# Spectral layers: the order of sum and split behind the second transform, and the rest's sum at the step's end

## The chip, the cores and the metric

One NeuronCore of a Trainium2 chip runs the whole program. The metric is the device time of one execution in microseconds. The engines are TensorE (PE in the profile, matrix products), VectorE (DVE), ScalarE (ACT), GpSimd (POOL) and SyncE (SP, which here only issues transfers). Each works off its own queue in order. Matrix products are written into PSUM, eight banks of 512 float32 per partition; ScalarE and VectorE read them from there.

## The reference, cut to what matters

Two inputs of 4096 tokens with 640 features go through a Fourier transform over tokens and features, a two-layer network on the complex spectrum in four blocks of 160 features, and the inverse transform. A gated feed-forward layer on the same tokens is mixed in.

```python
Xf = rfft2(x, axes=(1, 2))                     # x: (2, 1, 4096, 640)
z = Xf.reshape(B, H, Wf, 4, 160); zr, zi = z.real, z.imag
hr = zr @ w1[0] - zi @ w1[1] + b1[0]           # per block
hi = zi @ w1[0] + zr @ w1[1] + b1[1]
hr, hi = relu(hr), relu(hi)
or_ = hr @ w2[0] - hi @ w2[1] + b2[0]
oi_ = hi @ w2[0] + hr @ w2[1] + b2[1]
or_, oi_ = softshrink(or_, 0.01), softshrink(oi_, 0.01)
a = irfft2(or_ + 1j * oi_, s=(H, W), axes=(1, 2))
b = (gelu(x @ w_gate) * (x @ w_up)) @ w_down
g = sigmoid((x * gate_w).sum(-1, keepdims=True))
out = g * a + (1 - g) * b
```

The kernel takes a complex product as three real ones, for which it needs the sum of real and imaginary part beside the parts themselves. [...]

## The kernel before, in words

The program has three stages in time: the gated layer's first products, with the first transform between them; the spectral layers; and the second product of the gated layer, with the inverse transform and the output. The change lies in the spectral layers and in the last piece of the first stage, which prepares them.

The spectrum is cut into 16 chunks of 256 frequencies (eight for each input; chunk (0, 0), the second in order, has 258 and is called wide), and each chunk into its four blocks. A step is one block of one chunk: 64 steps in all. Of a block's 160 features 128 are the main part, and the remaining 32 of all four blocks together make a tile of 128, called the rest, which is treated once for a chunk and goes through memory to be read back block by block (zl).

fwd2 is the second half of the forward transform. Four products of TensorE fill one PSUM bank, pz, with real and imaginary parts (pr[:, 0] and pr[:, 1], 256 columns each). ScalarE rounds both into the high part z (high, L292 by the profile), and copies the second component into a buffer zt (L1030). VectorE subtracts the high part from the bank for the low part (low, L295) and adds the bank's first component to zt (L1033). fwd2 returns a function that splits that sum into zs, high on ScalarE and low on VectorE.

main_z calls fwd2 for a step's main part, one step ahead of its use; rest calls it for the rest and calls the returned function at once, then hands the parts to st, which puts stores off into a list (late) that flush issues on SP's queue at the start of the next step. zl_load, two steps ahead of use, reads them back on the same queue.

mlp1 is the first layer: products of zs into a bank (copied to kc by ScalarE, L1118), products of z, two additions hs on VectorE (L1125), then the function that main_z returned for the next step (so zs of the next step is split here), then relu and split of hs into h (L1081 on ScalarE, L1082 on VectorE), the last 32 features (L1131 on ScalarE, L1132 on VectorE), and in the end their split (L1135, L1136 and L1137), which mlp1 returns as a function called more. mlp2 is the second layer (m on ScalarE, y on VectorE). y_split splits y after every second step, its second half on GpSimd; inv1 is the inverse transform's first product, also after every second step, whose results go from PSUM to the buffer is, half of them by ScalarE (L1198), half by VectorE (L1200).

Nothing plans the order: each engine takes its instructions in the order of the code. One pass i of the loop over the steps issues, in this order: a load of the next chunk (in some steps), the flush of late, rest (once a chunk, in steps 4 ch - 3, two steps earlier for the last chunk), zl_load, main_z of step i + 1, mlp1 of step i, mlp2 of step i - 1, more of step i, inv1 of an earlier pair of steps if i is odd, y_split if i is even. The first chunk's rest is called in the last piece of the first stage.

Buffers come from pools with names: tiny (15 buffers of 1280 bytes a partition), small (17 of 2560), big (29 of 5120) and bank (8 PSUM banks). A tile takes a buffer that an earlier one has left; if the work on that one isn't over, the first writer waits. Where two engines touch the same tile or the same bank, semaphores keep them in the code's order.

## Time and profile before

| | |
|---|---|
| median of 3 runs | 2449.84 us (2448.95 to 2451.41) |
| profiled execution, its time | 2452.71 us |
| its span, first to last instruction | 2450.9 us |
| granted TensorE clock, mean | 0.996 |
| busy: TensorE, VectorE, ScalarE, GpSimd | 98%, 81%, 60%, 7% |
| stretch 1330 to 1742 us (spectral layers): TensorE, VectorE, ScalarE, GpSimd busy | 391.06, 343.70, 324.12, 77.20 of 412 us |

The profile is one execution on the chip. A row of the timeline gives start, duration (both us), engine, line, operation, the tiles written and read, their shape, and in brackets how long the engine had been idle before it and which instruction of another engine ended that. A row of the waits gives who waited for whom, the sum in us, how often, and the longest. The engines are named PE, DVE, ACT, POOL and SP; PEld is TensorE's loading of weights, which overlaps its products. L292 and L295 are the lines of the helpers high and low, L314 of the helper for a group of products, so such rows are told apart by their tiles.

### The profile page before, as it was taken

The page shows a single profiled execution, that of the slowest core. Times are in us where ns is not written, and L with a number is a line of the kernel's source. Part 1 is how long each engine was busy: PE and PEld are TensorE (multiplying, and loading weights), DVE is VectorE, ACT ScalarE, POOL GpSimd, SP SyncE. Part 2 cuts the span into 40 slices and gives each one's busy share as a digit, 9 for nine tenths or more (in the row PEclk, how much of TensorE's full clock was granted, in tenths as well). Part 3 has the DMA queues.
Part 4 walks back from the last instruction along what each step waited for, and adds up shares of the span by engine and source line. Part 5 has one row for each costly group of instructions (what it writes and reads, how often), then busy time and mean ns, then how long its engine had stood idle before and what let it go on. Part 6 is the DMA issues. An engine that isn't in the chain of part 4 may idle for free.

```text
span 2450.9 us, 50023 instructions
## 1 busy us (share of the span) xinstructions
PE 2413.5 (98%) x17983; PEld 2394.3 (98%) x17983; DVE 1984.5 (81%) x4191; ACT 1477.0 (60%) x3368; POOL 169.3 (7%) x270
## 2 busy tenths in 40 slices
PE   9999999999999999999999999999999999999999
PEld 9999999999999999999999999998899999999999
DVE  7777778777778888888757888888888988888887
ACT  5544456655556666666546777777745555555554
POOL 0111110000000000000001121211000000000000
PEclk9999999999999999999999999999999999999999
DMA  5666576777777768677765566668964455555443
GB/s 214 243 233 228 221 257 210 260 253 251 259 260 247 255 227 271 234 272 239 250 246 173 171 196 187 200 194 258 319 187 150 151 152 159 168 162 160 152 145 104
DMA packets 341314, 521.78 MB, mean 213 GB/s; under 512 B 28862, under 2 KB 217926, under 8 KB 341066
## 3 DMA queue, kind: packets, MB, share of 16 engines
q1 hardware_dynamic: 321002, 465.30, 57.7%
q0 software_dynamic: 20064, 53.29, 6.0%
q8 instruction: 142, 2.33, 0.4%
q14 instruction: 106, 0.87, 0.1%
HBM read 323.17 MB, written 195.30 MB: 212 GB/s over the span
## 4 chain that ended last, share of the span: by engine, by line
PE 86%; DMA 4%; DVE 4%; ACT 3%; issue 1%; SPq 1%; DVEq 0%; ACTq 0%
PE bank L580 73%; PE bank L314 7%; PE bank L711 2%; PE bank L834 1%; DMA zl<-zl 1%; PE bank L1018 1%; DMA sc<-scr 1%; DMA scr<-is 1%; DVE hs L1125 1%; ACT h L1081 1%; ACT ys L292 1%; DVE zt L1033 1%; ACT z L292 1%; DVE h L1082 1%; DMA xraw<-in_xT_dram 0%
## 5 line engine op out<-in xcount | busy, mean ns | idle before, releaser
L580 PE MATMUL bank<-xo,w 128*128 128x320 f32 (+1 forms) x9000 | 1252.5, 298 | 4.5 <-ACT u L607 3.6
L580 PEld LDWEIGHTS bank<-xo,w 128*128 128x128 f32 x9000 | 1221.8, 189 | 6.1 <-ACT u L607 3.8
L580 PE MATMUL bank<-wx,ho 128*128 128x320 f32 x4608 | 634.1, 300 | 3.4 <-DMA wx<-wdf 3.4
L580 PEld LDWEIGHTS bank<-wx,ho 128*128 128x128 f32 x4608 | 629.5, 189 | 4.3 <-DMA wx<-wdf 4.1
L295 DVE TENSOR_TENSOR ho<-hraw,ho 128x640 fp32r<-128x640 f32 (+3 forms) x384 | 194.4, 541 | 28.7 <-ACT ho L292 26.2
L292 ACT ACTIVATE ho<-hraw 128x640 fp32r<-128x640 f32 x320 | 169.0, 571 | 41.5 <-PE bank L580 31.3
L607 ACT ACTIVATE u<-bank 128x320 f32<-128x320 f32 (+1 forms) x250 | 107.5, 430 | 139.8 <-PE bank L580 133.6
L657 DVE TENSOR_TENSOR u<-bank,u 128x320 f32<-128x320 f32 (+1 forms) x165 | 80.1, 485 | 87.1 <-ACT u L607 86.1
L295 DVE TENSOR_TENSOR xs<-xr,xs 64x640 fp32r<-64x640 f32 x128 | 105.0, 820 | 47.0 <-ACT xs L292 43.7
L836 DVE TENSOR_TENSOR as<-bank,as 64x320 f32<-64x320 f32 x256 | 113.8, 484 | 25.6 <-ACT as L835 23.8
L295 DVE TENSOR_TENSOR xo<-xraw,xo 128x640 fp32r<-128x640 f32 (+1 forms) x155 | 125.1, 807 | 8.5 <-ACT xo L292 6.6
L314 PE MATMUL bank<-wm,h 128*128 128x320 f32 (+1 forms) x792 | 130.7, 301 | 0.1
L607 ACT ACTIVATE p<-bank 128x320 f32<-128x320 f32 (+1 forms) x125 | 54.1, 433 | 119.8 <-PE bank L580 61.8
L835 ACT ACTIVATE as<-bank 64x320 f32<-64x320 f32 x256 | 96.6, 426 | 31.7 <-PE bank L834 28.6
L292 ACT ACTIVATE xo<-xraw 128x640 fp32r<-128x640 f32 (+1 forms) x155 | 111.7, 721 | 5.9 <-DMA xraw<-in_xT_dram 4.1
L314 PEld LDWEIGHTS bank<-wm,h 128*128 128x128 f32 (+1 forms) x792 | 113.1, 188 | 1.5 <-ACT wt L1118 0.4
L1419 ACT ACTIVATE bank<-bank 128x320 f32<-128x320 f32 x31 | 13.1, 422 | 168.3 <-PE bank L580 168.3
L1413 DVE SCALAR_TENSOR_TENSOR uu<-bank,gs,uu 128x320 f32<-128x320 f32 x193 | 102.7, 546 | 13.0 <-PE bank L580 9.5
L1385 DVE SCALAR_TENSOR_TENSOR uu<-bank,gs,uu 128x320 f32<-128x320 f32 x120 | 57.8, 545 | 48.9 <-ACT uu L1384 48.8
L292 ACT ACTIVATE xs<-xr 64x640 fp32r<-64x640 f32 x128 | 93.4, 730 | 2.8 <-DMA hD<-h 0.7
L608 ACT ACTIVATE h<-bank 128x320 f32<-128x320 f32 (+1 forms) x165 | 71.2, 432 | 36.0 <-PE bank L580 33.0
L607 ACT ACTIVATE pb<-bank 128x320 f32<-128x320 f32 x80 | 35.0, 437 | 88.7 <-PE bank L580 88.6
(188 smaller groups left out, 3590.6 us busy)
## 6 DMA issues: line engine op xcount, KB each, us to landing
xo<-xD SPq DMA_DIRECT2D x96, 640.0 KB
xraw<-in_xT_dram SPq DMA_DIRECT2D x158, 320.0 KB
hD<-h SPq DMA_DIRECT2D x128, 320.0 KB
hraw<-hD SPq DMA_DIRECT2D x128, 320.0 KB
xD<-xo POOLq DMA_DIRECT2D x48, 640.0 KB, 4.3
sc<-scr SPq DMA_DIRECT2D x65, 320.0 KB
xr<-in_x_dram SPq DMA_DIRECT2D x64, 320.0 KB
scr<-as SPq DMA_DIRECT2D x64, 320.0 KB
```

The costliest lines, as they stand in the source:

```text
L292: nc.scalar.activation(dst, src, AF.Copy, scale=scale)
L295: eng.tensor_sub(dst, src, hi.bitcast(F32))
L314: nc.tensor.matmul(dst, l, by_two(r), start=i == 0, stop=i == len(ops) - 1)
L580: nc.tensor.matmul(dst, l, by_two(r), start=first and i == 0, stop=i == len(ops) - 1, skip_group_check=True)
L607: copy = lambda d, s_: nc.scalar.activation(d, s_, AF.Copy)
L608: gelu = lambda d, s_: nc.scalar.activation(d, s_, AF.Gelu_apprx_tanh)
L657: nc.vector.tensor_add(u4, C, u4)
L711: nc.tensor.matmul(acc, l, by_two(r), start=first and i == 0, stop=i == 2, skip_group_check=True)
L835: nc.scalar.activation(stg[hi, cs], pa[lo, :320], AF.Copy)
L836: nc.vector.tensor_add(stg[hi, cs], pa[hi, :320], stg[hi, cs])
L1385: nc.vector.scalar_tensor_tensor(uu[n2][:, cs], po[:, :320], gs[b][:, k, n2:n2 + 1], uu[n2][:, cs], op0=OP.mult, op1=OP.add)
L1413: nc.vector.scalar_tensor_tensor(dst, x, g, dst, op0=OP.mult, op1=OP.add)
```

## The change

In fwd2, where a sum is wanted, ScalarE's copy of the second component and VectorE's addition of the first are issued ahead of the split of z, not behind its two halves. The returned function takes the engine of the low part as an argument. rest no longer calls it at once: it puts a function into a list, later, which splits the rest's sum with the low part on GpSimd and then puts off its two stores; the loop over the steps calls it behind more and ahead of inv1. For the first chunk it is called right after rest, in the first stage, and there both halves of the rest's sum share one small buffer instead of taking two tiny ones.

```diff
@@ fwd2
             zz, pr = [z[h][:, :, :F] for h in range(2)], pz.rearrange("p (r n) -> p r n", r=2)
-        high(zz[0], pr)
         if zs:
             t = part_of(b, c, 0)
             t4 = t[:, :F].rearrange("p (e n) -> p e n", e=2)[..., :P] if F > CH else t[:, :F]
             nc.scalar.activation(t4, pr[:, 1], AF.Copy)
+            nc.vector.tensor_add(t4, pr[:, 0], t4)
+        high(zz[0], pr)
         low(zz[1], pr, zz[0])
-        if zs:
-            nc.vector.tensor_add(t4, pr[:, 0], t4)
         if wide(b, c):
...
-        return lambda: split(zs[0][:, :F], zs[1][:, :F], t[:, :F])
+        return lambda eng=nc.vector: split(zs[0][:, :F], zs[1][:, :F], t[:, :F], eng)
+
+    later = []
 
     def rest(b, c):
 
         F = width(b, c)
         z = zmid(b, c, [P, 2, 2, F], F32R, name="zz")
-        zs = [tiny([P, F], F32R, name="zs") for h in range(2)]
-        fwd2(b, c, 4 * P, [z[:, h] for h in range(2)], zs)()
+        first = (b, c) == chunks[0]
+        zs = small([P, 2, F], F32R, name="zs") if first else None
+        zs = [zs[:, h] if first else tiny([P, F], F32R, name="zs") for h in range(2)]
+        sums = fwd2(b, c, 4 * P, [z[:, h] for h in range(2)], zs)
         d = zld[b][c]
         for h in range(2):
             st(dr(d, 3 * CW * h, [[6 * CW, P], [CW, 2], [1, F]]), z[:, h].bitcast(F32))
-            st(dr(d, 3 * CW * h + 2 * CW, [[6 * CW, P], [1, F]]), zs[h].bitcast(F32))
+
+        def end():
+            sums(nc.gpsimd)
+            for h in range(2):
+                st(dr(d, 3 * CW * h + 2 * CW, [[6 * CW, P], [1, F]]), zs[h].bitcast(F32))
+        later.append(end)
@@ first stage
     at(last, 0, rest, *chunks[0])
+    at(last, 0, lambda: later.pop()())
     at(last, 2, zl_load, *chunks[0], 0)
@@ loop over the steps
         if i < S:
             more()
+        while later:
+            later.pop()()
         if 0 <= i - 2 < S - 1 and steps[i - 2][2] % 2:
             inv1(steps[i - 2][0], steps[i - 2][1], steps[i - 2][2] // 2)
```

## The prediction, made before the change was built

> **What bounds the kernel now.** I read the page first, then the waits of the whole span, then the spectral layers instruction by instruction. The page says that TensorE is busy nearly always:

> ```profile
> span 2450.9 us, 50023 instructions
> PE 2413.5 (98%) x17983; PEld 2394.3 (98%) x17983; DVE 1984.5 (81%) x4191; ACT 1477.0 (60%) x3368; POOL 169.3 (7%) x270
> ```

> That is an average over stages. The waits show who waits for whom in the spectral layers (columns: us in total, times, longest); all engines first, then TensorE alone:

> ```profile
> ACT zs L292 <- DVE zt L1033: 66.2, 73, 1.2
> ...
> ACT h L1081 <- DVE hs L1125: 16.1, 61, 1.3
> ...
> DVE z L295 <- ACT zt L1030: 14.6, 32, 0.8
> ...
> DVE zz L295 <- ACT zt L1030: 8.1, 13, 1.4
> ...
> ACT u L607 <- DMA zl<-zs: 3.9, 1, 3.9
> ```

> ```profile
> PE bank L314 <- DVE hs L1132: 11.3, 25, 0.6
> PE bank L314 <- DMA zl<-zl: 4.1, 2, 2.9
> PE bank L580 <- ACT u L607: 3.6, 1, 3.6
> ...
> PE bank L314 <- ACT kc L1118: 2.4, 10, 0.5
> PE bank L314 <- DVE zt L1033: 2.4, 10, 0.3
> ```

> Two things are to be seen. TensorE does wait for ScalarE and VectorE here, 16.1 us in all (11.3 + 2.4 + 2.4), while ScalarE's waits in this stage are for VectorE, and in the steady steps none is for TensorE. And the subtraction of z (L295) waits for the copy zt, 32 + 13 times, though it does not read zt. Both read the same bank of PSUM: the two engines take turns at a bank in the order of the program, even where both only read.

> One step of the layers, ScalarE and then VectorE (start, duration):

> ```profile
> 1473.32 0.41 ACT L1135 ACTIVATE hl<-hs 64x256 fp32r<-64x256 f32 x1
> 1473.63 0.41 ACT L1136 ACTIVATE hl<-hs 64x256 fp32r<-64x256 f32 x1
> ...
> 1474.57 0.59 ACT L292 ACTIVATE z<-bank 128x512 fp32r<-128x512 f32 x1
> 1475.05 0.38 ACT L1030 ACTIVATE zt<-bank 128x256 f32<-128x256 f32 x1
> ...
> 1476.51 0.42 ACT L292 ACTIVATE zs<-zt 128x256 fp32r<-128x256 f32 x1 [0.82 <-DVE zt L1033]
> 1477.17 0.63 ACT L1081 ACTIVATE h<-hs 128x512 fp32r<-128x512 f32 x1 [0.24 <-DVE hs L1125]
> ```

> ```profile
> 1474.49 0.89 DVE L1200 COPY is<-bank 128x320 f32<-128x320 f32 x2
> 1475.46 0.69 DVE L295 TENSOR_TENSOR z<-bank,z 128x512 fp32r<-128x512 f32 x1
> 1476.06 0.41 DVE L1033 TENSOR_TENSOR zt<-bank,zt 128x256 f32<-128x256 f32 x1
> 1476.39 0.75 DVE L1125 TENSOR_TENSOR hs<-bank,kc 128x256 f32<-128x256 f32 x2
> ```

> Call the start of ScalarE's first read of the bank T (1474.57). The subtraction starts at T+0.89, 0.03 after zt ends (1475.43); the addition follows at T+1.49, the two hs additions at T+1.82, and h, which lets the rest of the step run, 0.78 later. From h to the next T ScalarE works without a wait. So one loop through ScalarE and VectorE sets the pace: what happens between T and the hs additions is on the path. ScalarE's wait of 0.82 for zt, large in the list, is not: when zs is done (1476.93), ScalarE must still wait for hs.

> **The change, part by part.** First, the new order: copy zt, add (VectorE), round z (ScalarE), subtract (VectorE). All four touch one bank. If the turns hold, the rounding must now wait for the addition, so the bank passes ScalarE, VectorE, ScalarE, VectorE: three handovers instead of one, and the copy and the rounding no longer run back to back. Behind the waiting rounding stand kc, zs and h on ScalarE; behind the waiting subtraction the hs additions. I take 0.03 for each handover.

> There are 62 such places in the loop over the steps (read from the code: main_z is called once in each of steps 1 to 62): 30 follow the two inv1 copies (even steps from 4), 15 have rest ahead of them, 17 have neither.

> The plain place, after y_split:

> ```profile
> 1480.94 0.58 ACT L292 ACTIVATE z<-bank 128x512 fp32r<-128x512 f32 x1
> 1481.42 0.37 ACT L1030 ACTIVATE zt<-bank 128x256 f32<-128x256 f32 x1
> ```

> ```profile
> 1480.44 0.82 DVE L295 TENSOR_TENSOR ys<-y,ys 128x640 fp32r<-128x640 f32 x1 [0.23 <-ACT ys L292]
> 1481.82 0.69 DVE L295 TENSOR_TENSOR z<-bank,z 128x512 fp32r<-128x512 f32 x1 [0.55 <-ACT zt L1030]
> ...
> 1482.76 0.75 DVE L1125 TENSOR_TENSOR hs<-bank,kc 128x256 f32<-128x256 f32 x2
> ```

> Before: hs at T+1.82. After: copy to T+0.38, addition T+0.41 to T+0.82 (VectorE has been free since T+0.32), rounding T+0.85 to T+1.43, subtraction from T+1.46, and hs 0.61 behind its start, since one VectorE instruction starts 0.08 before the last ends: T+2.07. Cost 0.25 us, 17 times: **+4.3**.

> After the inv1 copies VectorE is not free at T+0.41: its copies end at 1475.38, T+0.81, and with the same overlap the addition starts at T+0.73. Rounding T+1.17 to T+1.75, subtraction T+1.78, hs T+2.39 instead of T+1.82: 0.57 us, 30 times: **+17.1**. (Without that overlap 0.65, or +19.5.) Before, the subtraction had to wait until T+0.89 anyway, so these copies cost nothing; now they are exposed.

> Second, the step with rest:

> ```profile
> 1493.06 0.58 ACT L292 ACTIVATE zz<-bank 128x512 fp32r<-128x512 f32 x1
> 1493.54 0.37 ACT L1030 ACTIVATE zt<-bank 128x256 f32<-128x256 f32 x1
> 1495.05 0.42 ACT L292 ACTIVATE zs<-zt 128x256 fp32r<-128x256 f32 x1 [1.15 <-DVE zt L1033]
> 1495.38 0.58 ACT L292 ACTIVATE z<-bank 128x512 fp32r<-128x512 f32 x1
> ```

> ```profile
> 1493.94 0.69 DVE L295 TENSOR_TENSOR zz<-bank,zz 128x512 fp32r<-128x512 f32 x1 [0.54 <-ACT zt L1030]
> ...
> 1496.32 0.69 DVE L295 TENSOR_TENSOR z<-bank,z 128x512 fp32r<-128x512 f32 x1 [0.39 <-ACT zt L1030]
> ...
> 1497.26 0.74 DVE L1125 TENSOR_TENSOR hs<-bank,kc 128x256 f32<-128x256 f32 x2
> ```

> Here the 1.15 of ScalarE's wait is on the path, for z stands behind it; hs starts at T+4.20 (T = 1493.06). After: copy to T+0.38, addition to T+0.82, rounding of zz T+0.85 to T+1.43, the main copy to T+1.71, zz's subtraction from T+1.46, the main addition T+2.07 to T+2.48, rounding T+2.51 to T+3.09, subtraction T+3.12, hs T+3.73. Gain 0.47 us, 15 times: **-7.1**.

> The rounding of rest's sum moves to the step's end, between L1136 and the inv1 copies on ScalarE. L1135 and L1136 start 0.31 apart, so it pushes the next T by 0.31. That place is one with inv1 copies, where VectorE, which sets the start of the addition, is not pushed: it is free at T+0.42 of the later T. I cost it at nothing; uncovered it is 15 x 0.31 = 4.7 us.

> The low part goes to GpSimd, and both stores of zs move behind it on SP's queue, ahead of the inv1 stores and the loads of zl:

> ```profile
> 1493.29 1.56 POOL L295 TENSOR_TENSOR ys<-y,ys 128x640 fp32r<-128x640 f32 x1 [9.52 <-PE bank L1102]
> ```

> ```profile
> 1501.65 1.25 SPq L272 DMA_DIRECT2D scr<-is  x2
> 1503.07 1.64 SPq L1061 DMA_DIRECT2D zl<-zl  x3
> ```

> GpSimd's price for 256 elements lies between 1.56 x 256/640 = 0.62 and 1.56 us; I take 0.62, the work being per element. With h at T+4.51 (1497.57), L1136 2.21 behind it as above and 0.30 more, zs is rounded by about 1500.5 and the low part is done by about 1501.1, before SP issues the inv1 stores now. The loads of zl behind it then wait for the stores to land. What hides that is more than a whole step between the loads and their use. Nothing, then; uncovered, TensorE would wait as it does at zl<-zl above, up to 2.9 a time.

> Third, the first rest takes its zs from the small buffers. In the row above u waited 3.9 for the store of zs, and TensorE 3.6 for u: u needed the tiny buffer that zs held. That wait should go: **-3.6** at most, 0 at least if another buffer is then late; I take all of it, since the store that u waited for is no longer in those buffers. At the layers' end TensorE waits 4.1 for zl; a slower loop could swallow up to that. I take nothing, because those loads stand behind stores of the loop's own results.

> Sum: 4.3 + 17.1 - 7.1 - 3.6 = **+10.7 us** on the profiled execution (2452.71, its span 2450.9). It lies 2.9 above the median of the runs, 2449.84; the difference carries over, so **2460.5**.

> The one thing no row shows is a ScalarE read behind a VectorE read of one bank; the rows show the other direction. [...]

> **The rivals.** (1) *The rounding does not wait for the addition*, only the subtraction for the rounding. Then zt ends at T+0.38, z at T+0.86, hs starts near T+1.50, 0.32 sooner, and rest's place gains about 1.8. The loop would give back over 16.1 us, but TensorE's waits above are 16.1, and below them it is the bound: -16.1 - 3.6 = -19.7, **2430**. It decides if ScalarE may read behind VectorE freely. Against it: the 45 waits of a subtraction for a copy that it does not read. (2) *TensorE hides it*: at 98% busy it might be the true bound, so that the loop's extra time falls into its shadow. Only -3.6 is left: **2446**, within the measurement's tolerance. Against it: ScalarE's and VectorE's steps are back to back, and TensorE waits for them. (3) *The late zs stores* make zl late for a matmul in each of the 15 chunks, 1 to 2.9 us each, on top of the sum: 2475 to 2504. Against it: the slack of a step.

> **How the numbers follow.** My forecast gets 0.78, rival 1 0.10, rival 2 0.08, rival 3 0.04. The forecast's own ends: 0.57 or 0.65 at the inv1 places (+14.3 or +16.7 before the first rest), 0 to 3.6 gained there, up to 4.1 swallowed at the end: +6.6 to +16.7, 2456 to 2467. To leave out no more than 2 in 10 the range goes from **2450 to 2468**, into rival 2 below. About 0.2% (4.9 us) is what a measurement of this kernel tells from no change. Slower by more: 0.78 (the forecast nearly whole, and rival 3); within it 0.11 (rival 2, the forecast's low end); faster 0.11.

> **What would show it.** Right: zt's addition starts within 0.05 of zt's copy at the plain places; a new wait of ScalarE's z for DVE zt, some 0.45 at a plain place and 0.8 behind inv1 copies; zs's wait for zt gone, with h's wait for hs grown in its place; rest's place shorter by about 0.5; a chunk of four steps about 0.9 longer (2 x 0.57 + 0.25 - 0.47); TensorE's wait for L1132 grown; u's wait for zl<-zs gone. Wrong: z rounded directly behind the copy with no wait (rival 1), or a loop as long as before, or TensorE waiting for zl<-zl in the middle of the layers.

## The result, and the profile after

| | before | after |
|---|---|---|
| median of 11 runs each | 2450.17 us (2447.67 to 2451.41) | 2456.23 us (2453.83 to 2458.34) |
| ratio, 95% interval | | 1.0026 (1.0017 to 1.0036) |
| profiled execution, its time | 2452.71 us | 2454.23 us |
| its span | 2450.9 us | 2452.4 us |

The change makes the kernel slower, by 6.06 us; 2460.5 was predicted. The two profiled executions differ by only 1.5 us in span, and that pair needs a word: before's lies 2.5 above its median and after's 2.0 below. Further down a cause is argued for that.

The page of after begins almost as before's did. TensorE is busy 99% of the time, so the average tells nothing:

```profile
span 2452.4 us, 50055 instructions
PE 2415.7 (99%) x17983; PEld 2388.7 (97%) x17983; DVE 1980.7 (81%) x4175; ACT 1476.4 (60%) x3368; POOL 181.1 (7%) x286
```

The waits of all engines after the change (in total, times, longest), and below them TensorE's own:

```profile
ACT h L1089 <- DVE hs L1133: 52.9, 64, 1.5
...
ACT z L292 <- DVE zt L1030: 40.3, 60, 1.1
...
ACT zz L292 <- DVE zt L1030: 7.8, 15, 0.9
```

```profile
PE bank L314 <- DVE hs L1140: 15.4, 25, 0.7
PE bank L314 <- ACT kc L1126: 7.1, 14, 0.6
PE bank L580 <- DMA wx<-wdf: 2.4, 2, 2.0
...
PE bank L314 <- DMA zl<-zl: 0.6, 1, 0.6
```

ScalarE's 66.2 us of waiting in front of zs are gone. In their place the rounding of z waits for the addition to zt, 60 times, and h waits for hs 52.9 us instead of 16.1. TensorE waits longer for hs (15.4 instead of 11.3) and for kc (7.1 instead of 2.4). Its wait for zl, 4.1 before, is down to 0.6, and u's wait for zl<-zs is not in the list any more.

A plain place after the change, ScalarE and then VectorE (T is 1479.88 here):

```profile
1479.88 0.36 ACT L1029 ACTIVATE zt<-bank 128x256 f32<-128x256 f32 x1
1480.73 0.60 ACT L292 ACTIVATE z<-bank 128x512 fp32r<-128x512 f32 x1 [0.49 <-DVE zt L1030]
...
1482.75 0.63 ACT L1089 ACTIVATE h<-hs 128x512 fp32r<-128x512 f32 x1 [0.84 <-DVE hs L1133]
```

```profile
1480.27 0.43 DVE L1030 TENSOR_TENSOR zt<-bank,zt 128x256 f32<-128x256 f32 x1
1481.36 0.69 DVE L295 TENSOR_TENSOR z<-bank,z 128x512 fp32r<-128x512 f32 x1 [0.66 <-ACT z L292]
1481.97 0.74 DVE L1133 TENSOR_TENSOR hs<-bank,kc 128x256 f32<-128x256 f32 x2
```

The bank goes from engine to engine as written: addition at T+0.39, rounding 0.03 behind the addition's end, subtraction 0.03 behind the rounding's, hs at T+2.09.

Where the 1.5 us of the profiled pair come from is read off two rows of each kernel: the first h of the layers and the h of step 62 (the last but one). First before, then after:

```profile
1325.31 0.63 ACT L1081 ACTIVATE h<-hs 128x512 fp32r<-128x512 f32 x1 [1.06 <-DVE hs L1125]
...
1742.26 0.63 ACT L1081 ACTIVATE h<-hs 128x512 fp32r<-128x512 f32 x1 [0.25 <-DVE hs L1125]
```

```profile
1319.92 0.63 ACT L1089 ACTIVATE h<-hs 128x512 fp32r<-128x512 f32 x1 [1.39 <-DVE hs L1133]
...
1751.61 0.63 ACT L1089 ACTIVATE h<-hs 128x512 fp32r<-128x512 f32 x1 [0.84 <-DVE hs L1133]
```

The first stage is 5.39 us shorter. The loop from the first h to that of step 62 takes 431.69 instead of 416.95, 14.74 more. And from there to the end of the span it takes 700.79 instead of 708.64, 7.85 less. The sum of the three is the 1.5.

### The profile page after: what moved, and what is told of

It reads as the page before. It is cut to its first block, busy times and chain, and to the rows that moved or that the text cites. A ratio compares the mean times of both kernels' runs of the same rounds, so it can differ in the third digit from the quotient of the medians.

```text
span 2452.4 us, 50055 instructions
## 1 busy us (share of the span) xinstructions
PE 2415.7 (99%) x17983; PEld 2388.7 (97%) x17983; DVE 1980.7 (81%) x4175; ACT 1476.4 (60%) x3368; POOL 181.1 (7%) x286
## 4 chain that ended last, share of the span: by engine, by line
PE 81%; issue 6%; DMA 4%; DVE 4%; ACT 3%; SPq 1%; POOL 0%; ACTq 0%; DVEq 0%; POOLq 0%
PE bank L580 68%; PE bank L314 8%; PE bank L711 2%; PE bank L834 1%; DMA zl<-zl 1%; DVE hs L1133 1%; PE bank L1018 1%; DMA f<-in_f_dram 1%; ACT h L1089 1%; DMA wx<-wdf 1%; DMA scr<-is 1%; DVE zt L1030 1%; DMA xraw<-in_xT_dram 0%; DMA sc<-scr 0%; ACT kc L1126 0%
## 5 line engine op out<-in xcount | busy, mean ns | idle before, releaser
L580 PE MATMUL bank<-xo,w 128*128 128x320 f32 (+1 forms) x9000 | 1250.4, 297 | 0.7 <-ACT p L607 0.7
L580 PEld LDWEIGHTS bank<-xo,w 128*128 128x128 f32 x9000 | 1220.0, 189 | 2.0 <-ACT p L607 1.2
L580 PE MATMUL bank<-wx,ho 128*128 128x320 f32 x4608 | 632.5, 299 | 3.6 <-DMA wx<-wdf 2.4
L580 PEld LDWEIGHTS bank<-wx,ho 128*128 128x128 f32 x4608 | 627.8, 189 | 4.7 <-DMA wx<-wdf 2.9
L295 DVE TENSOR_TENSOR ho<-hraw,ho 128x640 fp32r<-128x640 f32 (+3 forms) x384 | 194.4, 541 | 25.4 <-ACT ho L292 23.4
L292 ACT ACTIVATE ho<-hraw 128x640 fp32r<-128x640 f32 x320 | 168.9, 571 | 37.6 <-PE bank L580 31.1
L607 ACT ACTIVATE u<-bank 128x320 f32<-128x320 f32 (+1 forms) x250 | 107.4, 430 | 135.9 <-PE bank L580 132.0
L295 DVE TENSOR_TENSOR xs<-xr,xs 64x640 fp32r<-64x640 f32 x128 | 105.0, 820 | 46.7 <-ACT xs L292 43.3
L295 DVE TENSOR_TENSOR xo<-xraw,xo 128x640 fp32r<-128x640 f32 (+1 forms) x155 | 125.0, 807 | 8.7 <-ACT xo L292 6.8
L314 PE MATMUL bank<-wm,h 128*128 128x320 f32 (+1 forms) x792 | 129.4, 299 | 0.6 <-DVE zz L295 0.6
L607 ACT ACTIVATE p<-bank 128x320 f32<-128x320 f32 (+1 forms) x125 | 54.1, 432 | 118.7 <-PE bank L580 61.6
L292 ACT ACTIVATE xo<-xraw 128x640 fp32r<-128x640 f32 (+1 forms) x155 | 111.7, 721 | 5.3 <-DMA xraw<-in_xT_dram 4.1
L314 PEld LDWEIGHTS bank<-wm,h 128*128 128x128 f32 (+1 forms) x792 | 111.7, 186 | 2.1 <-DVE zz L295 0.9
L292 ACT ACTIVATE xs<-xr 64x640 fp32r<-64x640 f32 x128 | 93.4, 730 | 2.2 <-DMA hD<-h 0.4
L607 ACT ACTIVATE pb<-bank 128x320 f32<-128x320 f32 x80 | 34.9, 437 | 89.3 <-PE bank L580 89.3
```

The lines of the kernel that those rows point to most:

```text
L292: nc.scalar.activation(dst, src, AF.Copy, scale=scale)
L295: eng.tensor_sub(dst, src, hi.bitcast(F32))
L314: nc.tensor.matmul(dst, l, by_two(r), start=i == 0, stop=i == len(ops) - 1)
L580: nc.tensor.matmul(dst, l, by_two(r), start=first and i == 0, stop=i == len(ops) - 1, skip_group_check=True)
L607: copy = lambda d, s_: nc.scalar.activation(d, s_, AF.Copy)
```

## The experiments

Each was compared with the kernel before on the same chip; the intervals are 95%. What the change does falls into three parts: the new order in fwd2, the late split of rest's sum, and the small buffer of the first rest. The first and the last are run alone; the late split is run together with the small buffer, which acts in the first stage, so that the loop shows the late split.

**The new order alone**

```diff
 # the kernel before, fwd2
-        high(zz[0], pr)
         if zs:
             ...
             nc.scalar.activation(t4, pr[:, 1], AF.Copy)
-        low(zz[1], pr, zz[0])
-        if zs:
             nc.vector.tensor_add(t4, pr[:, 0], t4)
+        high(zz[0], pr)
+        low(zz[1], pr, zz[0])
```

> Kernel before with fwd2's new order alone; rest splits its sum at once on VectorE as before, with tiny buffers. Theory (engines take turns at the bank, so the rounding waits for the addition): 0.27 x 17 at plain places, 0.59 x 30 behind the inv1 copies, -0.14 x 15 at rest's places: +20 us in the loop, no gain in the first stage, 3 to 7 us of it swallowed by the transfers at the layers' end: +13 to +20, 2463 to 2470. Rival (the cost comes from the late split of rest's sum on GpSimd, the order costs nothing): 2450, within 3 us.

Measured: 2468.80 against 2450.18, ratio 1.0081 (1.0067 to 1.0094). The order costs 18.6 us by itself.

**All but the new order**

```diff
 # the kernel after, fwd2
+        high(zz[0], pr)
         if zs:
             ...
             nc.scalar.activation(t4, pr[:, 1], AF.Copy)
-            nc.vector.tensor_add(t4, pr[:, 0], t4)
-        high(zz[0], pr)
         low(zz[1], pr, zz[0])
+        if zs:
+            nc.vector.tensor_add(t4, pr[:, 0], t4)
```

> The change without its new order: fwd2 as before, rest's split at the step's end with the low part on GpSimd, small buffer for the first. Theory: at rest's place hs starts at T+2.75 instead of T+4.20, 15 x -1.45, and rest's rounding behind L1136 pushes the loop by 0.31, 15 times: -17 in the loop, of which TensorE's waits there (16) let through 12 to 16; the first stage -5.4 (3.6 of wait and 1.8 of the half clock behind it); the transfers at the layers' end may take up to 7 back: 2430 to 2440. Rival (the late split is what costs): 2456 or more.

Measured: 2428.39 against 2450.18, ratio 0.9916 (0.9902 to 0.9929): 21.8 us faster than before, somewhat more than expected. So the change is a good one and a bad one in one diff.

The two don't add up in the loop: alone the order adds 20.7 us there and the late split takes 15.0 away, 5.7 together, where the whole change adds 14.7. In a steady chunk of four steps, from one rounding of rest's zz to the next (26.61 us before), the order adds 1.42, the late split takes 1.15 away, and both together add 1.07. The step with rest shows why. The start of ScalarE's first read (T) and of the hs additions on VectorE, with the order alone, with the late split alone, and with both (the kernel after):

```profile
1503.18 0.37 ACT L1029 ACTIVATE zt<-bank 128x256 f32<-128x256 f32 x1
```

```profile
1507.36 0.75 DVE L1124 TENSOR_TENSOR hs<-bank,kc 128x256 f32<-128x256 f32 x2
```

```profile
1454.65 0.58 ACT L292 ACTIVATE zz<-bank 128x512 fp32r<-128x512 f32 x1
```

```profile
1457.40 0.74 DVE L1134 TENSOR_TENSOR hs<-bank,kc 128x256 f32<-128x256 f32 x2
```

```profile
1492.85 0.36 ACT L1029 ACTIVATE zt<-bank 128x256 f32<-128x256 f32 x1
1493.71 0.60 ACT L292 ACTIVATE zz<-bank 128x512 fp32r<-128x512 f32 x1 [0.49 <-DVE zt L1030]
```

```profile
1496.63 0.75 DVE L1133 TENSOR_TENSOR hs<-bank,kc 128x256 f32<-128x256 f32 x2
```

hs started at T+4.20 before. With the order alone it is T+4.18, with the late split alone T+2.75, and with both T+3.78. The late split is worth 1.45 us where the old order stands and 0.40 where the new one does: with the new order ScalarE stands still for the addition anyway. Of the 1.05 lost, 0.31 come back, because the rounding at the step's end, which pushes the next T by 0.31, is covered with the new order (below). That is 0.74 of the 0.80 by which a chunk does not add up.

**Is it the addition ahead of the subtraction, or the rounding's wait?** In this kernel ScalarE copies and rounds back to back, and VectorE adds before it subtracts:

```diff
 # the kernel after, fwd2
             nc.scalar.activation(t4, pr[:, 1], AF.Copy)
-            nc.vector.tensor_add(t4, pr[:, 0], t4)
         high(zz[0], pr)
+        if zs:
+            nc.vector.tensor_add(t4, pr[:, 0], t4)
         low(zz[1], pr, zz[0])
```

> The change with ScalarE's copy of zt and rounding of z back to back, then the addition, then the subtraction: the addition is still ahead of the subtraction, but the rounding no longer waits for it. Theory (the handovers cost): hs starts at T+1.83 at plain places as before, so as without the new order: 2430 to 2440. Rival (the addition ahead of the subtraction is what delays hs): as the change, 2456.

Measured: 2428.70, ratio 0.9915 (0.9902 to 0.9927). Its plain place, ScalarE and then VectorE:

```profile
1468.29 0.37 ACT L1029 ACTIVATE zt<-bank 128x256 f32<-128x256 f32 x1
1468.56 0.59 ACT L292 ACTIVATE z<-bank 128x512 fp32r<-128x512 f32 x1
```

```profile
1469.18 0.42 DVE L1032 TENSOR_TENSOR zt<-bank,zt 128x256 f32<-128x256 f32 x1 [0.55 <-ACT z L292]
1469.52 0.68 DVE L295 TENSOR_TENSOR z<-bank,z 128x512 fp32r<-128x512 f32 x1
1470.12 0.75 DVE L1134 TENSOR_TENSOR hs<-bank,kc 128x256 f32<-128x256 f32 x2
```

Both orders on VectorE bring hs at T+1.82 (before) or T+1.83. With one handover of the bank the addition may go first at no cost; it is the two further handovers that are paid for.

**Does the rounding wait for the addition because of the bank?** The four products are done a second time into a bank of their own, which the copy and the addition read; the order is that of after.

```diff
 # the kernel after, fwd2
+        pzs = bank() if zs else pz
+        for px in (pzs, pz) if zs else (pz,):
             ... the four products, into px
-            nc.scalar.activation(t4, pr[:, 1], AF.Copy)
-            nc.vector.tensor_add(t4, pr[:, 0], t4)
+            nc.scalar.activation(t4, prs[:, 1], AF.Copy)     # prs: pr's view of pzs
+            nc.vector.tensor_add(t4, prs[:, 0], t4)
```

> The changed kernel, with copy and addition reading a second bank that TensorE fills with the same four products once more (work added, 78 times about 0.9 us of TensorE). Only the order inside a step counts. Theory (the rounding waits because of the bank): ScalarE's z starts 0.28 behind zt, without a wait for VectorE's zt, and the subtraction right behind z; the total is TensorE's, 2480 to 2520. Rival (it waits for the addition itself, or for zt's buffer): z still starts 0.85 behind T, with ScalarE's wait for DVE zt as in the changed kernel.

Measured, one execution: 2471.03, less than expected. The total says nothing on the wait, as TensorE has four products more per place and is the bound then: it is busy for all 412.00 us from 1330 to 1742, where it is for 387.26 in after. The step with rest does (T is 1502.01), ScalarE and then VectorE:

```profile
1502.01 0.36 ACT L1035 ACTIVATE zt<-bank 128x256 f32<-128x256 f32 x1
1502.27 0.58 ACT L292 ACTIVATE zz<-bank 128x512 fp32r<-128x512 f32 x1
```

```profile
1502.40 0.42 DVE L1036 TENSOR_TENSOR zt<-bank,zt 128x256 f32<-128x256 f32 x1
1502.88 0.69 DVE L295 TENSOR_TENSOR zz<-bank,zz 128x512 fp32r<-128x512 f32 x1
```

The rounding starts at T+0.26, ahead of the addition (T+0.39), where after has it at T+0.86 (1493.71). The order is the same, and only the bank that copy and addition read is another. So the wait is for the bank. What the run shows is an order that this program keeps at a bank; what the chip would do without it, no run here shows.

**Is GpSimd worth anything?** The kernel with back-to-back reads, and rest's low part on VectorE again:

```diff
 # the kernel with back-to-back reads, rest
         def end():
-            sums(nc.gpsimd)
+            sums()
```

> The kernel with copy and rounding back to back, but the low part of rest's sum on VectorE at the step's end instead of GpSimd. Theory (the loop has room there: VectorE's inv1 copies end before ScalarE's later T): 0 to +0.3 a chunk, 0 to +5: 2428 to 2434. Rival (taking it from VectorE is where the gain lies): 0.42 a chunk and the wait for ScalarE, +6 to +15: 2435 to 2444.

Measured: 2426.42 against 2449.81, ratio 0.9904 (0.9888 to 0.9921). Its interval overlaps that of the kernel with GpSimd (0.9902 to 0.9927): no gain from moving the low part can be told.

**Another place for the late split**: right behind the main sum's split, where ScalarE stands waiting for hs, and not at the step's end.

```diff
 # the kernel with back-to-back reads, mlp1 and the loop
         sums()
+        while later:
+            later.pop()()
         relu_split(h[0], h[1], hs)
 ...
             more()
-        while later:
-            later.pop()()
```

> The kernel with copy and rounding back to back, with rest's sum split not at the step's end but right behind the main part's sum, ahead of h, where ScalarE waits for VectorE's hs additions (0.8 us idle). Theory: the rounding of 0.42 fits into that wait, the push of 0.31 at the step's end is gone: 15 x 0.31 = 4.7 less in the loop, of which TensorE's and the transfers' waits let through some: 2423 to 2428. Rival (TensorE and the transfers bound it by now): 2428, no change.

Measured: 2425.87, ratio 0.9900 (0.9886 to 0.9914). A chunk of four steps goes from 25.46 to 25.16 us (from rest's copy zt to the next: 1454.95 to 1480.41, and 1455.24 to 1480.40), 0.30 where 0.31 was expected; in the total it can't be told from the two kernels above. All three beat both the kernel before and the changed one, by about 1%.

**The first rest's buffer alone**

```diff
 # the kernel before, rest
-        zs = [tiny([P, F], F32R, name="zs") for h in range(2)]
+        first = (b, c) == chunks[0]
+        zs = small([P, 2, F], F32R, name="zs") if first else None
+        zs = [zs[:, h] if first else tiny([P, F], F32R, name="zs") for h in range(2)]
```

> Kernel before with the small buffer for the first rest's zs alone. Theory: the stall of 3.6 us goes and with it the 3.4 us at half clock behind it (1.8 us): -5.4, 2444.8; no half clock before 1600 us in the profile. Rival 1 (the half clock is by chance or has another cause): -3.6, 2446.6, half clock still there. Rival 2 (another buffer is late in its place): no change, 2450.

Measured: 2442.44 against 2450.18, ratio 0.9970 (0.9958 to 0.9982), 7.7 us. The first h is 5.18 us earlier in its profile, near the 5.4 that after showed and well over the 3.6 of TensorE's stall. The other 2.5 lie behind the first stage, where no line of the edit is; the table further down shows how much the layers' end varies. The windows of before name what the 3.6 leaves of those 5.4 (us of the window; busy time of PE, PEld, DVE, ACT, POOL; then PEclk, the share of the full TensorE clock that was granted; DMA share, GB/s); after's stand below:

```profile
1285.00:1290.00 5.00, 1.44 (x8) 1.22 (x7) 1.17 (x3) 1.24 (x3) 0.00 (x0) 0.93 0.49 161
1290.00:1295.00 5.00, 5.00 (x29) 5.00 (x28) 4.90 (x19) 2.95 (x13) 0.63 (x1) 0.73 0.01 2
```

```profile
1285.00:1290.00 5.00, 5.00 (x39) 5.00 (x38) 4.88 (x20) 3.69 (x14) 1.00 (x2) 1.00 0.41 134
1290.00:1295.00 5.00, 5.00 (x39) 5.00 (x38) 3.71 (x14) 3.10 (x9) 0.77 (x2) 1.00 0.49 171
```

TensorE is idle for most of the first window before, and in the second it does 29 products where 39 fit, at a clock of 0.73. The lost clock is 0.07 x 5 + 0.27 x 5 = 1.7 us, and 3.6 + 1.7 = 5.3.

**Does the lower clock follow from the idle time?** To before are added 26 products that nobody reads, in front of the one that stalls. They fill the idle time; what u waits for stays as it is.

```diff
 # the kernel before, in the last piece of the first stage
+            if key == keys[-1] and t == groups[2][0]:
+                wb, (l, r) = half(), prod(w["s4"], x_of(o, "b22"))[0]
+                for k in range(26):
+                    nc.tensor.matmul(wb, l, by_two(r), start=True, stop=True)
             run(X, prod(w["s4"], x_of(o, "b22")), first=False)
```

> Kernel before, with 26 products whose result nobody reads put ahead of the product that stalls 3.6 us at the first rest, each about 0.14 us, so that TensorE works through the stall instead of idling (work added, none left out). Theory (the half clock follows from the idle time): the stall is filled, no half clock before 1600 us, and h of the first step comes 1.5 to 1.9 earlier than in the kernel before though the wait of u for the store is as long. Rival (the half clock comes at that time whatever TensorE does, or from the wait itself): half clock at 1290 as before, no gain.

Measured, one execution: 2445.24, first h 1.66 us earlier than before. The windows of this kernel, and ScalarE's wait:

```profile
1285.00:1290.00 5.00, 4.91 (x37) 4.67 (x36) 1.16 (x3) 1.20 (x4) 0.00 (x0) 1.00 0.49 161
1290.00:1295.00 5.00, 5.00 (x39) 5.00 (x38) 4.90 (x19) 3.14 (x14) 1.25 (x3) 1.00 0.02 5
```

```profile
ACT u L607 <- DMA zl<-zs: 3.9, 1, 3.9
```

u waits as long as before, and yet the clock stays full. The other traces agree: the half clock near 1290 stands in all three with TensorE's stall there (before, the order alone, the later load below) and in none of the nine without it. So this stall was paid twice: once for its length (3.6 us), and once for the half clock behind it (1.7).

**The layers' end: does a transfer's place decide?** Before, with one load of constants issued a step later:

```diff
 # the kernel before, the transfers of the last steps
-           S - 4: [(c_load, 0), wl(1, 3)],
-           S - 3: [(v_load, 1), (h_load, 0, 0), wl(1, 4)],
+           S - 4: [wl(1, 3)],
+           S - 3: [(c_load, 0), (v_load, 1), (h_load, 0, 0), wl(1, 4)],
```

> Kernel before, with the first c_load (two loads of the inverse transform's input) issued one step later, so that the last load of zl on SP's queue no longer stands behind it. Theory (the end of the layers in the kernel before loses 4.1 us of stall at zl and 3.4 us to the half clock behind it, and the slower loop of the change swallows that): the stall at zl and the half clock near 1750 go, 3 to 7 us less: 2443 to 2447. Rival (the transfers' volume bounds the layers' end, whatever their order): 2450, a stall elsewhere in its place.

Measured: 2447.70 against 2449.81, ratio 0.9991 (0.9982 to 0.9999), 2.1 us and less than expected. TensorE's wait for zl goes from 4.1 to 2.4 us, and its wait for wx at the same end takes 3.1 instead of 3.4. The wait for zl behind the h of step 62 is gone, but the one ahead of it has grown from 1.2 to 2.0 us, and a half clock stands there, from 1738 (in before from 1747). So theory and rival were each right in part, and the run does not settle what the place is worth.

**Both together**: the split in the gap and the later load.

```diff
 # the kernel with the split behind the main sum, the transfers of the last steps
-           S - 4: [(c_load, 0), wl(1, 3)],
-           S - 3: [(v_load, 1), (h_load, 0, 0), wl(1, 4)],
+           S - 4: [wl(1, 3)],
+           S - 3: [(c_load, 0), (v_load, 1), (h_load, 0, 0), wl(1, 4)],
```

> The two that were faster together: copy and rounding back to back with rest's sum split ahead of h, and the first c_load one step later. Theory (they act at different places): the loop's gain and some 2 us at the layers' end: 2422 to 2426. Rival (the end is bound by the transfers' volume once the loop is faster): 2426 or more, no better than the first alone.

Measured: 2425.30 against 2447.55, ratio 0.9903 (0.9886 to 0.9919). The load's place adds nothing that can be told apart.

## Where the layers' end took its time

All profiled executions but the one with the second bank, in us. The late split and all kernels with back-to-back reads have the first rest's small buffer too. The lost clock is the sum over seventy windows of 1 us from the h of step 62 on, each with 1 minus its granted clock; the waits are all of TensorE's that are listed for the same seventy.

| kernel | to first h | first h to h of step 62 | from there to the end | lost clock | waits | end without both |
|---|---|---|---|---|---|---|
| before | 1325.3 | 417.0 | 708.6 | 5.1 | 6.3 | 697.2 |
| after | 1319.9 | 431.7 | 700.8 | 0.0 | 4.4 | 696.4 |
| order alone | 1327.7 | 437.7 | 701.8 | 1.7 | 4.0 | 696.1 |
| late split, old order | 1319.1 | 401.9 | 706.4 | 3.4 | 6.4 | 696.6 |
| first rest's buffer | 1320.1 | 415.7 | 705.4 | 3.4 | 4.9 | 697.1 |
| back-to-back reads | 1319.4 | 400.1 | 703.8 | 0.0 | 6.3 | 697.5 |
| the same, VectorE | 1319.9 | 400.2 | 705.5 | 1.7 | 5.9 | 697.9 |
| the same, split in the gap | 1320.9 | 398.4 | 704.9 | 1.7 | 5.8 | 697.4 |
| later load | 1324.3 | 417.6 | 704.5 | 1.7 | 5.1 | 697.7 |
| split in the gap, later load | 1319.6 | 397.4 | 706.7 | 1.7 | 6.6 | 698.4 |
| filled stall | 1323.7 | 416.6 | 703.2 | 1.7 | 5.1 | 696.4 |

The end varies by 7.8 us, and by 2.3 when lost clock and waits are taken off. So most of it is these two, and lost clock is the larger part of the difference between before and after: 5.1 of 7.85. This is an account, no experiment: no kernel here takes the half clock at the end away and leaves all else. The column of the loop holds such stretches too: one of 1.7 us in before, in the order alone, in the late split and in each of the last four rows, none in the others.

One such stretch of before in full, with the stall ahead of it (windows of 1 us, then TensorE's timeline):

```profile
1677.00:1678.00 1.00, 0.49 (x2) 0.30 (x2) 1.00 (x3) 1.00 (x4) 0.00 (x0) 1.00 0.98 365
1678.00:1679.00 1.00, 0.48 (x2) 0.49 (x2) 0.69 (x3) 1.00 (x3) 0.00 (x0) 0.71 1.05 388
1679.00:1680.00 1.00, 0.96 (x5) 0.67 (x5) 0.66 (x1) 0.43 (x1) 0.44 (x1) 0.50 1.06 376
1680.00:1681.00 1.00, 1.00 (x6) 1.00 (x6) 0.00 (x0) 0.82 (x2) 1.00 (x1) 0.50 1.11 292
1681.00:1682.00 1.00, 1.00 (x7) 1.00 (x7) 0.92 (x2) 0.05 (x1) 0.94 (x3) 0.58 1.03 340
1682.00:1683.00 1.00, 1.00 (x12) 1.00 (x11) 0.46 (x2) 0.80 (x3) 0.16 (x1) 1.00 0.89 351
```

```profile
1678.52 3.33 PE L1018 MATMUL bank<-f,sc 128*128 128x128 f32 x12 [1.02 <-DMA sc<-scr]
```

The clock goes to one half and back: 0.29 + 0.50 + 0.50 + 0.42 = 1.71 us lost, which is 3.42 us at half. All losses in the table are about one, two or three times this 1.71. One stretch is 0.0007 of the mean clock.

Such a stretch also comes in one execution and not in the next. Each execution's time stands with its mean granted clock: ten of before, taken beside the first four experiments, and the eleven of after.

| mean clock | before, us | after, us |
|---|---|---|
| 1.000 | | 2453.83, 2454.23 (the profiled one) |
| 0.999 | 2445.65, 2447.18 | eight, 2455.70 to 2458.34 |
| 0.998 | 2447.32 | 2458.21 |
| 0.997 | 2448.63, 2449.63, 2451.31, 2452.42 | |
| 0.996 | 2450.73, 2451.32 (and the profiled one, 2452.71) | |
| 0.995 | 2453.60 | |

The lower the clock, the longer the time. (The eleven of before in the result have no listed clock.) In the mean, before runs at 0.9971 here (0.9974 over all 32 executions with a listed clock) and after at 0.9990. The difference, 0.0016 to 0.0019 of 2450, is 3.9 to 4.7 us, which no wait shows; 1.7 of it is the first stage's. The profiled pair, 0.996 and 1.000, happened to show more of it than most.

## Why the prediction was right, and where its sizes were off

**The turns at the bank: right, and by their sizes.** The rounding's wait was 0.49 at a plain place (about 0.45 forecast) and 0.80 behind inv1's copies (0.8). hs came at T+2.09 (T+2.07), T+2.41 (T+2.39) and, in rest's step, T+3.78 (T+3.73). The place behind the copies in after, T at 1485.89 on ScalarE, then VectorE:

```profile
1485.89 0.37 ACT L1029 ACTIVATE zt<-bank 128x256 f32<-128x256 f32 x1
1487.07 0.60 ACT L292 ACTIVATE z<-bank 128x512 fp32r<-128x512 f32 x1 [0.80 <-DVE zt L1030]
```

```profile
1485.81 0.89 DVE L1208 COPY is<-bank 128x320 f32<-128x320 f32 x2
1486.62 0.41 DVE L1030 TENSOR_TENSOR zt<-bank,zt 128x256 f32<-128x256 f32 x1
...
1488.30 0.75 DVE L1133 TENSOR_TENSOR hs<-bank,kc 128x256 f32<-128x256 f32 x2
```

The overlap that was chosen (addition at T+0.73) is there. With the measured prices the loop's sum is 17 x 0.27 + 30 x 0.59 - 15 x 0.42 = +16.0; forecast was +14.3 and the trace has +14.7. Before's loop holds a half-clock stretch and after's none, which can hide up to 1.7 of the cost: 16.4 at most. A chunk of four steps is 1.07 longer (0.9 forecast).

No row of before showed ScalarE's read behind VectorE's: the forecast's wait of the rounding was the author's estimate, carried over from the other direction. It is shown now, by after (60 waits of z for the addition, 40.3 us in all) and by the second bank (the rounding at T+0.26, ahead of the addition). Rival 1 falls with both.

**Edits put at nothing: right.** GpSimd's subtraction took 0.73 us (0.62 taken), the zs stores behind it made no zl late in the middle of the layers (TensorE's one listed wait for zl, of 0.61, is at 1707.57), and rival 3 falls. Rest's rounding at the step's end was taken to be covered, since the place behind it has inv1's copies. It was: there T came 0.31 late and hs another 0.29 behind it, together 0.60 beside the 0.59 of the other such places, at 1500.86 against 1485.89.

**Rival 2 falls too.** TensorE does not hide the loop: the order alone makes the kernel 18.6 us slower, and the change without it runs in 2428.39 where the change with it takes 2456.23.

**The first rest: term mis-sized.** "-3.6 at most" was wrong. The stage gained 5.4, since the half clock behind the stall goes with the stall; the filled stall shows 1.66 of it alone. The row that said so, PEclk in the windows of the first stage, was not read.

**The layers' end: the step that failed.** "I take nothing", with "up to 4.1 swallowed" as the bound, put only the wait for zl at stake. The profiled pair gave back 7.85 there: 5.1 is lost clock, 1.9 are waits (zl 2.9 less, wx 1.0 less, others 2.0 more), and 0.8 is neither. The slower loop does seem to swallow the wait for zl: it is missing behind step 62 in the kernels with the new order, and 1.1 to 2.9 us long in all others whose load of constants stands in its old place. That loads stand behind the loop's own stores was no reason against it. But the larger part, the clock, was in no term and no bound. In the medians the end's share can't be read off and is what is left over: 6.06 + 5.39 - 14.74 = -3.3, of which the mean clocks explain 3.9 - 1.7 = 2.2 to 4.7 - 1.7 = 3.0. Behind which stalls of the profiled executions the clock fell is worked out in the last section; for executions without a trace it can't be read, so why before runs at the lower clock more often than after stays open. Before does have two long stalls that after lacks, 3.6 us in the first stage and 2.9 for zl.

So the forecast of +10.7 against +6.06 misses a gain of 1.8 at the first rest and one of 3.3 at the end, less 0.4 in the loop. The mechanism of the loop was right by its terms. That the total lay within the range is partly luck: the two misses went the same way, and the room for them had been left for other causes, a swallowed wait and rival 2.

## What to carry to other kernels

Where two engines read one PSUM bank, let each do all its reads in one go: here the two orders with one handover cost the same (hs at T+1.82 and T+1.83), while with three it came at T+2.09, and at T+2.41 where the second engine had other work queued (the wait 0.80 us, not 0.49). A large wait in the list was not the path here (66.2 us removed, and the loop slower), and a wait that two edits remove is gained once: the late split was worth 1.45 us a place with the old order and 0.40 with the new. And a stall of the bounding engine may be priced too low by its length (here 3.6 us of stall had 1.7 of lost clock behind it): read the granted clock behind it, and expect it to differ from one execution to the next (0.995 to 0.999 in ten of before).

## What was not expected of the hardware

The half clock. In these traces a stretch at a clock of 0.50 lasts 3.41 us or twice that and follows waits of TensorE, but the length of one stall does not decide: before shows it behind one of 1.02 us, and after has none at all though TensorE once waited 2.0 us for wx. Where it falls matters too. The stretches of one execution start whole multiples of 3.413 us apart (in before at 1289.30, 1678.42, 1746.68 and 1780.82, which is 114, 20 and 10 times 3.413; 491.52 over 144 gives the figure), so they can be laid on a grid of windows of that length. Below, all twelve traces are cut on such grids (in after, which has no such stretch, the grid is laid by the fall of its clock at 2454.35, behind the last instruction), and the windows at full clock, without those at the two ends of a span, are sorted by TensorE's busy time in them.

| TensorE busy, of 3.413 us | windows | the next one at half clock |
|---|---|---|
| up to 1.44 us | 17 | 17 |
| 1.54 to 1.91 us | 7 | 4 |
| 1.95 us or more | 8485 | 0 |
